# A Fourier filter feeding a gated feed-forward: the order of loads and stores in the prologue, changed

## The chip, the cores and the metric

The kernel runs on one core of one Trainium2 chip. The time is that of the device, in microseconds (us), as the median of several executions. One further execution is recorded by the hardware profiler; its views are what this document reads.

## The reference

The input x has 8 sequences (batches) of 3008 tokens with 256 features. Each feature's sequence goes through a real Fourier transform, is multiplied by a complex filter and is transformed back. The result, 24064 tokens in all, goes through a feed-forward layer with a product of two branches:

```python
X = np.fft.rfft(x, axis=1)
F = (filt_r + 1j * filt_i)[None, :, :]
y = np.fft.irfft(X * F, n=x.shape[1], axis=1)
x = y.reshape(B * S, D)                    # 24064 x 256
gate = np.maximum(x @ w_gate, 0.0)         # 256 -> 1536
val = x @ w_val
out = (gate * val) @ w_out                 # 1536 -> 256
```

## The kernel before

The length 3008 is split as 94 x 32, so that both transforms are matmuls of small tables. For one batch the work goes in four stages.

- **Stage A** (`items_a`, line 269, used for batches 0 and 1). x lies in two SBUF tiles XF[0] and XF[1], 4 MB of room in all, filled by `load_x` (line 172). One item multiplies 512 columns of XF with the table WA in float32 (two passes on PE, line 276) and ScalarE copies the result to a tile asb (line 279). After four items SP stores asb to a DRAM buffer Abuf (line 281). So 16 items make four stores ("quarters"). Batches 2 to 7 take another way: GpSimd loads x in chunks (`load_chunk`), adds and subtracts (`fold_chunk`), and `tiled_a` does smaller matmuls.
- **The bounce.** `load_at` (line 346) reads one quarter of Abuf back, transposed, into a quarter of the tile `at`. A forward transform of the next stage needs all four quarters.
- **Stage B.** `fwd` (line 355) multiplies `at` with the table F2 into PSUM (psX). `product` (line 368) multiplies psX with the filter's parts Ftr and Fti, on VectorE (line 379), or for the pairs in POOL_U by a copy on ScalarE (line 376) and a product on GpSimd (line 377). `inv` (line 382) transforms back with the tables I2t and I2u (line 393), ScalarE copies the result (line 400), and SP stores it to the buffer Dbuf (line 402). For batch 0 this is the loop `first_b`, with six indices i; in it, `amid` puts either filler matmuls or items of stage A of batch 1.
- **Stage C and the feed-forward.** `load_d` (line 421) reads a quarter of Dbuf into dC. `item_c` makes a block yT of 512 tokens. `gv` (line 458) computes val and gate of 128 of the 1536 features, and their product; `o_part` (line 475) multiplies with the output weights. A block takes 12 steps, and there are 47 blocks. Further work is attached to single steps by `at_step` (line 591): step s is feature group s mod 12 of block s div 12.

Every engine runs its instructions in the order in which the program writes them; there is no planner. Stage A and B of batch 1 therefore run where the code puts them: stage A in and after `first_b`, stage B at the steps in the list of line 617, counted from `end`, which is 51 for batch 1.

The prologue needs more than x. The tables I2t and I2u are made on PE from F2 and from the tile `tabs` (`make_back_t`, line 187; `make_back_u`, line 200). The filters are loaded on GpSimd's queue by `load_filters` (line 216, eight transfers, converting to bfloat16) and `load_own_filters` (line 226, the border rows); `place_filter` (line 233) then copies each to a second set of partitions, on VectorE and once on ScalarE. The weights come by `load_vg` (line 244, halves of val and gate) and `load_o`. XF is cleared by memsets first, since x fills only 94 of its rows' groups.

Three devices hold transfers back so that others go first. `hold_gpsimd` (line 255) makes GpSimd copy a few elements of a tile, and so wait for it, before it issues what follows. The load called `last` (line 571) reads the end of Dbuf on GpSimd's queue before the second half of the weights. And the little store `gate` (line 555) makes SP wait for the whole of `at` before it issues the loads of x of batch 1 (line 556).

`warm` (line 504) issues matmuls on a constant tile `junk` whose results nobody reads, to keep TensorE active.

Of the kernel before, what the change touches and what calls it, by code (L numbers as in the profile page):

```python
# [35 lines left out]
def _ap(t, offset_elems, ap_list):  # L36
    return dataclasses.replace(
        t, offset=t.offset + offset_elems, ap=[list(p) for p in ap_list]
    )
# [81 lines left out]
def kernel(  # L121
# [30 lines left out]
    pro = prologue.enter_context(tc.tile_pool(name="pro", bufs=1))  # L152

    Abuf = [dram.tile([NROW * N2, D], BF16, name=f"Abuf{b}") for b in range(B)]
    gate = dram.tile([32, 8], BF16, name="gate")
    Dbuf = [dram.tile([NROW * N2, D], BF16, name=f"Dbuf{b}") for b in range(B)]

    XF = [pro.tile([128, NX2 * D], FP32, name=f"XF{c}") for c in range(N2 // NX2)]
# [13 lines left out]
    def load_x(b, eng, cols):  # L172
        w = NX2 * D
        for c, c0, c1 in cols:
            for m in range(3):
                rows = min(32, B * N1 - (b * N1 + 32 * m))
                eng.dma_start(XF[c][m:m + 4 * rows - 3:4, c0:c1],
                              _ap(x, (b * N1 + 32 * m) * N2 * D + c * w + c0,
                                  [[N2 * D, rows], [1, c1 - c0]]))
# [7 lines left out]
    def make_back_t(q):  # L187

        psI = [ps.tile([128, 4, 64], FP32, tag=fft_tag(), name="psI") for _ in range(2)]
        for e in range(2):  # L190
            for a in range(2):
                for j in range(4):
                    nc.tensor.matmul(psI[e][64 * a:64 * a + 64, j],
                                     F2[64 * e:64 * e + 64, 12 * a + 4 * q + j, :],
                                     perm[64 * e:64 * e + 64], start=True, stop=True,
                                     tile_position=(64 * e, 64 * a))
        for e in range(2):
            nc.vector.tensor_copy(I2t[:, 8 * q + e:8 * q + 8:2, :], psI[e])
# [17 lines left out]
    def load_filters():  # L216

        for src, dst in FILT:
            for a in range(2):
                r, k1, n = a * 64, 1 + 24 * a, NG - 2 * a  # L220
                nc.gpsimd.dma_start(dst[r:r + 31:2, 0:n, :],
                                    _ap(src, k1 * D, [[N1 * D, 16], [1, n * D]]))
                nc.gpsimd.dma_start(dst[r + 1:r + 32:2, 0:n, :],
                                    _ap(src, (N1 - k1) * D, [[N1 * D, 16], [-D, n], [1, D]]))

# [18 lines left out]
    def load_vg(c0, c1):  # L244
        for (w_hbm, w_sb) in ((moe_w_val, WvT), (moe_w_gate, WgT)):
            nc.gpsimd.dma_start(w_sb[:, :, c0:c1],
                                _ap(w_hbm, c0, [[DFF, 128], [128 * DFF, 2], [1, c1 - c0]]))
# [7 lines left out]
    def hold_gpsimd(tile_):  # L255

        scr = sb.tile([128, 8], FP32, tag="scr", bufs=2)
        nc.gpsimd.tensor_copy(scr[:tile_.shape[0]], tile_)  # L258
# [123 lines left out]
    def inv(b, i, tags=None, cuts=CUTS):  # L382

        if i in cuts:
            dsbs[b] = i, sb.tile([128, 2, 4, D], BF16, tag="dsb", bufs=3, name="dsb")
        i0, dsb = dsbs[b]
        psD = [ps.tile([128, 2, D], FP32, tag=tags[a] if tags else fft_tag(), name="psD")
               for a in range(2)]
        for m in range(2):
            for k in range(2):  # L390
                for a in range(2):
                    for e in range(2):
                        nc.tensor.matmul(psD[a][64 * e:64 * e + 64, m],  # L393
                                         (I2t, I2u)[k][64 * a:64 * a + 64, 4 * i + 2 * m + e, :],
                                         tus[b, i, e, k][64 * a:64 * a + 64, m],
                                         start=(k == 0), stop=(k == 1),
                                         tile_position=(64 * a, 64 * e))
        o = 2 * (i - i0)
        for a in range(2):
            nc.scalar.copy(dsb[:, a, o:o + 2, :], psD[a])  # L400
        if i + 1 in cuts:
            nc.sync.dma_start(_ap(Dbuf[b], 2 * i0 * D, [[NG * D, 128], [NG // 2 * D, 2], [1, (o + 2) * D]]),
                              dsb[:, :, :o + 2, :])

    def first_b(amid):

        cuts = (0, 2, 4, 5, 6)
        for i in range(6):
            fwd(0, i)
            if i > 1:  # L410
                inv(0, i - 2, cuts=cuts)
            for e in range(2):
                product(0, i, e, 0)
                product(0, i, e, 1, pool=(i, e) in POOL_U)
            amid(i)
        inv(0, 4, cuts=cuts)
        inv(0, 5, cuts=cuts)

    dCs = {}
# [84 lines left out]
    def warm(n, cols=512):  # L504

        psJ = ps.tile([128, 512], FP32, tag=fft_tag(True), name="psJ")
        for i in range(n):
            nc.tensor.matmul(psJ[:, :cols], junk[:, 0:128], junk[:, :cols], start=True, stop=True)

    nc.sync.dma_start(WA, nc.inline_tensor(wa_h, name="dft_wa").ap())  # L510
    q = NX2 * D // 4
    nc.vector.memset(XF[0][:, 0:q], 0.0)
    nc.gpsimd.memset(XF[0][:, q:2 * q], 0.0)
    nc.vector.memset(junk, 1.0)
# [1 line left out]
    nc.gpsimd.memset(XF[0][:, 3 * q:], 0.0)  # L516
    nc.vector.memset(XF[1][:, 0:2 * q], 0.0)
    nc.gpsimd.memset(XF[1][:, 2 * q:], 0.0)
    load_x(0, nc.sync, ((0, 0, 2 * q), (0, 2 * q, 4 * q), (1, 0, 2 * q)))
    nc.sync.dma_start(F2, nc.inline_tensor(f2_h, name="dft_f2").ap())  # L520
    nc.sync.dma_start(tabs, nc.inline_tensor(tab_h, name="dft_tab").ap())
    load_x(0, nc.sync, ((1, 2 * q, 4 * q),))
    nc.sync.dma_start(WF, nc.inline_tensor(fold_h, name="dft_fold").ap())
    for (src, dst) in FILT:
        nc.vector.memset(dst[64:128, NG - 2:, :], 0.0)
    hold_gpsimd(XF[0][:, 2 * q - 8:2 * q])
    load_filters()
    load_own_filters()

    warm(11)  # L530
    for i, f in enumerate(items_a(0)):
        f()
        if i >= 13:
            make_back_t(i - 13)
        else:
            warm(1, 256)
        if i == 11:
            load_at(0, 0)
    for c in range(1, 4):
        load_at(0, c)  # L540
    for half in range(2):
        for a in range(2):
            place_filter(0, a, half, nc.vector.tensor_copy)
    for i in range(3):
        make_back_u(i)
        warm(6)
    warm(18)
    place_own()
    for half in range(2):
        for a in range(2):  # L550
            place_filter(1, a, half, nc.vector.tensor_copy if a or not half else nc.scalar.copy)
    place_nyq()
    hold_gpsimd(ats[0][0:32, NG - 1, 0:8])
    load_vg(0, DFF // 2)
    nc.sync.dma_start(gate, ats[0][0:32, NG - 1, 0:8])
    load_x(1, nc.sync, ((0, 0, 2 * q), (0, 2 * q, 4 * q), (1, 0, 4 * q)))

    early = items_a(1)
# [1 line left out]
    def amid(i):  # L560
        if i < 2:
            warm(3, 256)
        else:
            for _ in range(2 if i > 2 else 1):
                next(early)()

    turn["tags"], turn["side"] = ("fft", "psv", "psg"), "pso"
    first_b(amid)
    turn["tags"], turn["side"] = ("fft", "psv", "psg", "pso"), None
    load_d(0, 0, 1)  # L570
    nc.gpsimd.dma_start(pro.tile([1, D], BF16, tag="last", bufs=1, name="last"),
                        _ap(Dbuf[0], (N2 * NROW - 1) * D, [[D, 1], [1, D]]))
    load_vg(DFF // 2, DFF)
    load_o()
    for f in early:
        f()
    for h in range(2):
        item_c(0, h)
    prologue.close()
# [11 lines left out]
    def at_step(s, f):  # L591
        side.setdefault(s, []).append(f)

    for s, z in ((0, 1), (9, 2), (14, 3)):
        at_step(s, lambda z=z: load_d(0, z, z + 1))
    C_AT = (8, 10)
    at_step(2, clear_chunks)
    for b in range(1, B):
        end = (b * S // W - 1) * NFT + C_AT[0] - 5
        if b == 1:  # L600
            for c in range(4):
                at_step(3, lambda c=c: load_at(1, c))
        else:
            for j, e in enumerate((-74, -69, -64, -57)):
                l = end - 113 + NFT * j

                def next_x(b=b, j=j, l=l):
                    hold_gpsimd(yTs[l // NFT + 1][:, 0, 0:8])
                    load_chunk(b, j)
                    if j:  # L610
                        fold_chunk(b, j - 1)
                    if j == 3:
                        fold_chunk(b, j)
                at_step(l, next_x)
                at_step(end + e, lambda b=b, j=j: tiled_a(b, j))
            at_step(end + e + 4, lambda b=b: load_at_tiled(b))
        for i, l in enumerate((-35, -28, -25, -22, -16, -11, -4) if b == 1 else
                              (-40, -35, -28, -23, -16, -11, -4)):
            if i < 6:
                at_step(end + l, lambda b=b, i=i: fwd(b, i))  # L620
                for h in range(4):
                    at_step(end + l + h, lambda b=b, i=i, h=h: product(b, i, h // 2, h % 2))
            if i > 0:
                at_step(end + l, lambda b=b, i=i: inv(b, i - 1, ("psv", "psg")))
        at_step(end - 2, lambda b=b: load_d(b))
# [42 lines left out]
```

## Time and profile before

| what | value |
|---|---|
| time, median of 3 | 906.75 us (906.66 to 909.95) |
| the profiled execution | 907.27 us |
| its span | 905.5 us |
| PE busy | 875.3 us, 97% of the span |
| VectorE, ScalarE, GpSimd busy | 566.6, 498.6, 359.0 us |
| PE busy from 0 to 111 us | 92.8 us |
| PE busy from 111 to 905 us | 782.5 of 794 us |
| first matmul of stage A of batch 0 | 7.46 us |
| first forward transform of batch 0 | 33.44 us |
| first matmul of the feed-forward | 63.90 us |

In the profile, PE is TensorE's matmuls and PEld its weight loads, DVE is VectorE, ACT ScalarE, POOL GpSimd, SP SyncE. A name such as `psA L276` is the tile written and the line in the kernel. "DMA at<-Abuf" is the time between the issue of a transfer and its landing. In the windows, "DMA" is the mean busy share of the 16 DMA engines; it goes over 1 where packets overlap.

### The profile page before, as it was taken

Reading aid. Unit: us, or ns where it says so; the run is one execution under the profiler, and the core shown is the slowest. Engines: PE = TensorE matmul, PEld = TensorE weight load, DVE = VectorE, ACT = ScalarE, POOL = GpSimd, SP = SyncE. Lnnn points to the kernel's source line nnn. Section 1 sums busy time; section 2 is a strip of 40 time slices with the busy share of each in tenths; the row PEclk is TensorE's granted clock in tenths of the full one; section 3 lists DMA queues with packets and bytes.
Section 4 is the critical chain, followed back from the end, with each engine's and each line's share of the span. In section 5 each row is a group of like instructions: output and inputs, shape, how many; then the busy total and the mean of one; then the engine's idle time right before and its main releaser. Section 6 shows DMA issues by size and latency. Waiting matters only on the chain.

```text
span 905.5 us, 19111 instructions
## 1 busy us (share of the span) xinstructions
PE 875.3 (97%) x7096; PEld 512.1 (57%) x7217; DVE 566.6 (63%) x872; ACT 498.6 (55%) x891; POOL 359.0 (40%) x351
## 2 busy tenths in 40 slices
PE   8797899999999999999999999999999999999997
PEld 3343565556555665566655566556655556666665
DVE  2635776567665776657766677657766577655553
ACT  4474556555555555555655565655565555555552
POOL 4342667117680386614763166811768000000000
PEclk9899999999999999999999999999999999999999
DMA  9979337623475344663364533754346512331111
GB/s 254 245 219 220 101 95 177 141 80 109 122 175 118 90 126 122 141 134 112 96 161 128 119 98 101 182 116 100 108 136 158 116 31 82 78 75 36 37 32 51
DMA packets 113662, 109.17 MB, mean 121 GB/s; under 512 B 20290, under 2 KB 98370, under 8 KB 112834
## 3 DMA queue, kind: packets, MB, share of 16 engines
q1 hardware_dynamic: 91078, 81.72, 35.3%
q0 software_dynamic: 22176, 26.01, 11.7%
q8 instruction: 57, 0.93, 0.5%
q10 hardware_dynamic: 316, 0.22, 0.1%
q14 instruction: 35, 0.29, 0.1%
HBM read 61.93 MB, written 49.81 MB: 123 GB/s over the span
## 4 chain that ended last, share of the span: by engine, by line
PE 86%; DVE 4%; DMA 4%; ACT 3%; issue 1%; SPq 1%; POOL 0%; DVEq 0%; POOLq 0%
PE psG L464 25%; PE psO L483 25%; PE psV L464 24%; DVE prod L469 4%; PE psA L276 3%; PE psF L322 3%; ACT vsb L467 3%; PE psD L393 2%; PE psX L363 2%; PE psY L448 1%; DMA XF<-in_x_dram 1%; DMA dC<-Dbuf 1%; DMA Abuf<-asb 1%; DMA out_dram<-osb 0%; DMA at<-Abuf 0%
## 5 line engine op out<-in xcount | busy, mean ns | idle before, releaser
L469 DVE SCALAR_TENSOR_TENSOR prod<-psG,vsb 128x512 bf16<-128x512 f32 x564 | 389.0, 690 | 271.3 <-ACT vsb L467 265.8
L467 ACT CAST vsb<-psV 128x512 bf16<-128x512 f32 x564 | 333.0, 590 | 266.8 <-PE psV L464 211.7
L483 PE MATMUL psO<-WoT,prod 128*128 128x256 bf16 x2256 | 336.6, 273 | 1.5
L464 PE MATMUL psG<-yT,WgT 128*128 128x512 bf16 x1099 | 329.1, 379 | 7.4 <-DMA WgT<-in_moe_w_gate_dram 2.5
L464 PE MATMUL psV<-yT,WvT 128*128 128x512 bf16 x1037 | 316.9, 380 | 0.7 <-ACT yT L453 0.4
L483 PEld LDWEIGHTS <-prod 128*128 128x128 bf16 x2256 | 220.7, 98 | 143.4
L464 PEld LDWEIGHTS <-WgT 128*128 128x128 bf16 x1128 | 109.9, 98 | 136.9 <-DMA WgT<-in_moe_w_gate_dram 3.0
L464 PEld LDWEIGHTS <-WvT 128*128 128x128 bf16 x1128 | 98.1, 98 | 41.8 <-issue 30.4
L258 POOL CAST scr<-yT 128x8 f32<-128x8 bf16 x24 | 4.6, 191 | 265.8 <-ACT yT L453 265.8
L379 DVE TENSOR_TENSOR tt<-psX,Ftr 128x512 bf16<-128x512 f32 x96 | 65.0, 682 | 12.9 <-PE psX L363 12.9
L400 ACT CAST dsb<-psD 128x512 bf16<-128x512 f32 x96 | 51.5, 589 | 28.5 <-PE psD L393 28.4
L308 POOL TENSOR_TENSOR fold<-XP 128x1024 f32<-128x1024 f32 x24 | 56.5, 2356 | 25.1 <-PE psF L322 24.9
L489 ACT COPY osb<-psO 128x512 f32<-128x512 f32 x92 | 54.5, 593 | 20.6 <-PE psO L483 20.3
L379 DVE TENSOR_TENSOR uu<-psX,Fti 128x512 bf16<-128x512 f32 x89 | 60.6, 681 | 0.0
L309 POOL TENSOR_TENSOR XP<-XP 128x1024 f32<-128x1024 f32 x24 | 56.4, 2350 | 1.9
L295 POOL DMA_DIRECT2D XP<-in_x_dram x96 | 56.4, 592 | 0.9 <-issue 0.5
L453 ACT CAST yT<-psY 128x512 bf16<-128x512 f32 x47 | 27.6, 586 | 26.2 <-PE psY L448 26.2
L329 DVE CAST asb<-psF 128x512 bf16<-128x512 f32 x48 | 30.9, 686 | 17.3 <-PE psF L322 12.9
L329 ACT CAST asb<-psF 128x512 bf16<-128x512 f32 x48 | 25.8, 589 | 27.3 <-PE psF L322 27.3
L448 PE MATMUL psY<-M,dC 96*128 96x94 bf16 (+18 forms) x604 | 37.7, 198 | 1.1 <-DMA dC<-Dbuf 1.1
L455 DVE CAST yT<-psY 128x512 bf16<-128x512 f32 x47 | 32.0, 681 | 9.8 <-PE psY L448 9.8
L448 PEld LDWEIGHTS <-dC 96*128 96x128 bf16 x604 | 34.5, 97 | 4.6 <-DMA dC<-Dbuf 1.2
(66 smaller groups left out, 481.6 us busy)
## 6 DMA issues: line engine op xcount, KB each, us to landing
at<-Abuf SPq DMA_DIRECT2D x32, 384.0 KB
dC<-Dbuf SPq DMA_DIRECT2D x64, 192.0 KB
XP<-in_x_dram POOLq DMA_DIRECT2D x48, 256.0 KB, 5.9
Dbuf<-dsb SPq DMA_DIRECT2D x23, 512.0 KB
XP<-in_x_dram POOLq DMA_DIRECT2D x96, 96.0 KB, 2.7
Abuf<-asb SPq DMA_DIRECT2D x96, 96.0 KB
out_dram<-osb SPq DMA_DIRECT2D x70, 94.0 KB
XF<-in_x_dram SPq DMA_DIRECT2D x18, 256.0 KB
```

The costliest lines, as they stand in the source:

```text
L295: nc.gpsimd.dma_start(xp[r:r + 24, 0:4:2, :], _ap(x, (b * N1 * N2 + o) * D, [[N2 * D, 24], [47 * N2 * D, 2], [1, 512]]))
L308: tt(t, xp[:, 0:2], xp[:, 2:4], op=ALU.add)
L309: tt(xp[:, 2:4], xp[:, 0:2], xp[:, 2:4], op=ALU.subtract)
L329: copy(asf[:, :, q, :], banks[q])
L379: nc.vector.tensor_tensor(p, psX, filt, op=ALU.mult)
L400: nc.scalar.copy(dsb[:, a, o:o + 2, :], psD[a])
L448: nc.tensor.matmul(psY[:, o:o + w], dCs[b, n2 // 8][:, n2 % 8, h * 128:(h + 1) * 128], M1[:, n1:n1 + w], start=True, stop=True)
L464: nc.tensor.matmul(pt[:, :W], w[:, h, ft * 128:(ft + 1) * 128], yt[:, h, :], start=(h == 0), stop=(h == 1))
L467: nc.scalar.copy(vsb, psV[:, :W])
L469: nc.vector.scalar_tensor_tensor(prod, in0=psG[:, :W], scalar=0.0, in1=vsb, op0=ALU.max, op1=ALU.mult)
L483: nc.tensor.matmul(psO[:, t % 2], prods[ft][:, t * 128:(t + 1) * 128], WoT[:, ft, :], start=(ft == 0), stop=(ft == NFT - 1))
L489: copy(osb[:, t0 % 2:t % 2 + 1], psO[:, t0 % 2:t % 2 + 1])
```

## The change

It touches the prologue and the first steps of the feed-forward.

1. F2 and `tabs` are loaded on ScalarE's queue, at the start. The first filter transfer is issued on GpSimd ahead of its memsets; `load_filters` becomes a generator for this, and its other seven transfers follow when the first half of XF[1] has landed (before: when the first half of XF[0] had).
2. x of batch 0 is loaded in five pieces, the first two of half the size, with nothing between them on SP's queue.
3. Stage A of batch 0 runs without filler and without `make_back_t`, which follows after it with filler of its own.
4. The store `gate` is gone, so that the loads of x of batch 1 stand directly behind the loads of `at` on SP. On GpSimd, the hold on `at` and `load_vg` keep their place.
5. In `first_b`, items of stage A of batch 1 are spread 1, 1, 2, 1, 1 instead of 1, 2, 2, 2, the last one between the last two `inv`.
6. Two quarters of Dbuf are loaded at once, ahead of the other stores to Abuf. The loads of `at` of batch 1 are taken forward: quarter 0 before the rest of stage A, quarter 1 within it, quarters 2 and 3 at steps 0 and 1 (all four were at step 3).
7. The forward transforms of batch 1 stand at steps 11, 16, 23, 28, 35, 40 instead of 16, 23, 26, 29, 35, 40.

```diff
@@ load_filters
                                     _ap(src, k1 * D, [[N1 * D, 16], [1, n * D]]))
+                yield
                 nc.gpsimd.dma_start(dst[r + 1:r + 32:2, 0:n, :],
@@ first_b
         inv(0, 4, cuts=cuts)
+        amid(6)
         inv(0, 5, cuts=cuts)
@@ the prologue
+    q = NX2 * D // 4
     nc.sync.dma_start(WA, nc.inline_tensor(wa_h, name="dft_wa").ap())
-    q = NX2 * D // 4
+    nc.scalar.dma_start(F2, nc.inline_tensor(f2_h, name="dft_f2").ap())
+    nc.scalar.dma_start(tabs, nc.inline_tensor(tab_h, name="dft_tab").ap())
+    filters = load_filters()
+    next(filters)
...
-    load_x(0, nc.sync, ((0, 0, 2 * q), (0, 2 * q, 4 * q), (1, 0, 2 * q)))
-    nc.sync.dma_start(F2, nc.inline_tensor(f2_h, name="dft_f2").ap())
-    nc.sync.dma_start(tabs, nc.inline_tensor(tab_h, name="dft_tab").ap())
-    load_x(0, nc.sync, ((1, 2 * q, 4 * q),))
+    load_x(0, nc.sync, ((0, 0, q), (0, q, 2 * q), (0, 2 * q, 4 * q), (1, 0, 2 * q), (1, 2 * q, 4 * q)))
...
-    hold_gpsimd(XF[0][:, 2 * q - 8:2 * q])
-    load_filters()
+    hold_gpsimd(XF[1][:, 2 * q - 8:2 * q])
+    for _ in filters:
+        pass
     load_own_filters()
 
     warm(11)
     for i, f in enumerate(items_a(0)):
         f()
-        if i >= 13:
-            make_back_t(i - 13)
-        else:
-            warm(1, 256)
         if i == 11:
             load_at(0, 0)
     for c in range(1, 4):
         load_at(0, c)
+    for i in range(3):
+        make_back_t(i)
+        warm(6)
...
     for i in range(3):
         make_back_u(i)
         warm(6)
-    warm(18)
+    warm(6)
...
-    hold_gpsimd(ats[0][0:32, NG - 1, 0:8])
-    load_vg(0, DFF // 2)
-    nc.sync.dma_start(gate, ats[0][0:32, NG - 1, 0:8])
     load_x(1, nc.sync, ((0, 0, 2 * q), (0, 2 * q, 4 * q), (1, 0, 4 * q)))
@@ amid
-            for _ in range(2 if i > 2 else 1):
+            for _ in range((1, 1, 2, 1, 1)[i - 2]):
                 next(early)()
 
+    hold_gpsimd(ats[0][0:32, NG - 1, 0:8])
+    load_vg(0, DFF // 2)
@@ after first_b
-    load_d(0, 0, 1)
+    load_d(0, 0, 2)
...
-    for f in early:
+    load_at(1, 0)
+    for i, f in enumerate(early):
         f()
+        if i == 5:
+            load_at(1, 1)
@@ the steps
-    for s, z in ((0, 1), (9, 2), (14, 3)):
+    for s, z in ((9, 2), (14, 3)):
...
-            for c in range(4):
-                at_step(3, lambda c=c: load_at(1, c))
+            for c in range(2, 4):
+                at_step(c - 2, lambda c=c: load_at(1, c))
...
-        for i, l in enumerate((-35, -28, -25, -22, -16, -11, -4) if b == 1 else
-                              (-40, -35, -28, -23, -16, -11, -4)):
+        for i, l in enumerate((-40, -35, -28, -23, -16, -11, -4)):
```

More of the change, by code (lines that the diff above doesn't have):

```diff
@@ L154 @@
     Abuf = [dram.tile([NROW * N2, D], BF16, name=f"Abuf{b}") for b in range(B)]
-    gate = dram.tile([32, 8], BF16, name="gate")
     Dbuf = [dram.tile([NROW * N2, D], BF16, name=f"Dbuf{b}") for b in range(B)]
```

## The prediction

> **What bounds the kernel now.** I read the chain of waits in order of time first, because the page's totals (PE busy 97% of the span) hide the start. Its first 90 us:
>
> ```profile
> 24.41 5.40 DMA Abuf<-asb
> 29.83 3.48 DMA at<-Abuf
> ...
> 34.98 6.99 DMA XF<-in_x_dram
> ...
> 42.11 1.99 PE psA L276 x2
> ...
> 54.55 7.91 PE psA L276 x18
> ...
> 65.74 9.95 DMA dC<-Dbuf
> ...
> 85.84 1.79 issue
> ```
>
> Columns: start, length, what. Four transfers and a wait stand on the path. Then the windows (start:end, length, then busy time of PE, PEld, DVE, ACT, POOL, then PE clock, DMA share, GB/s):
>
> ```profile
> 0.00:33.40 33.40, 29.37 (x142) 11.37 (x143) 14.30 (x24) 15.11 (x21) 10.58 (x20) 1.00 0.92 254
> ...
> 38.30:42.10 3.80, 0.01 (x2) 0.02 (x1) 0.00 (x0) 2.05 (x4) 2.69 (x3) 0.76 1.11 310
> 42.10:54.60 12.50, 12.49 (x119) 5.34 (x120) 6.26 (x10) 8.56 (x16) 2.43 (x3) 0.80 0.78 281
> ...
> 63.90:87.60 23.70, 18.29 (x98) 8.82 (x100) 12.47 (x19) 10.45 (x18) 9.91 (x11) 1.00 1.17 233
> ...
> 111.00:905.00 794.00, 782.50 (x6467) 469.10 (x6580) 511.79 (x786) 441.54 (x795) 310.42 (x292) 1.00 0.43 108
> ```
>
> After 111 us PE is 98.6% busy and DMA share is 0.43: nothing there changes. All is decided before 111, where DMA is full in three stretches. Last, the list of waits from 63 to 111 us names what holds PE in the feed-forward part:
>
> ```profile
> PE psG L464 <- DMA WgT<-in_moe_w_gate_dram: 2.5, 1, 2.5
> PE psX L363 <- DVE uu L379: 2.2, 2, 1.1
> PE psX L363 <- issue: 1.8, 1, 1.8
> ```
>
> With 0.7 us for dC at 75.8, that is 7.2 us. The "issue" row is the end of the wait for `at` of batch 1: the trace's landing records put its last quarter at 87.54, the matmul at 87.63.
>
> **What the skill says.** "DMA: Bandwidth & Descriptors", section "Issuing engines are not separate DMA queues": another issuing engine saves only the issue time. Here that is 0.59 + 0.43 us of SP for F2 and tabs. Same page, "Queues, rings and completion order": each DMA engine goes round between queues packet by packet. The trace agrees: SP's x and POOL's filters land interleaved from 12 to 20 us. "TensorE: Matmul & The Clock Gate", section "What's actually happening": PE falls to half clock after an idle window of about 3.4 us. The trace agrees: after the 3.8 us wait one item of stage A took 1.99 instead of 0.86; after the 2.5 us wait at 70.1 PE ran on at its old pace.
>
> **Part 1, loads and stage A.** F2 and tabs go from SP's queue (7.76, 8.39) to the head of ACT's (about 0.7). Two issues of some 0.6 us delay ACT's table load (1.28 us); ACT's first copy came at 8.57 after 6.5 us idle, so they cost nothing, unless data came 4 us earlier. The first filter goes ahead of POOL's memsets: 0.65 us later for each (0.95, 0.95, 1.81 us), so the second quarter of XF is clear at about 2.4; SP reaches its load only after three issues of 0.6, at 3.8: hidden. The x loads become 15 instead of 12 issues, +1.8 us of SP, but F2 and tabs (1.0) are gone and the first chunk is half as big. The first three landed at 7.33 before; I put the first 384 KB at 6 and the whole of x at about 14.5 (last issue at 11.4 plus 3), against 18.98.
>
> PE's opening filler, 11 matmuls, runs from 2.53 to 6.85, so stage A starts at 6.9 instead of 7.46. Each item is 2 x 0.43; the 13 fillers (0.11 each) and the three groups of make_back_t (0.28 to 0.35) leave. 16 x 0.86 = 13.8, so the last item ends at 20.7 and its copy (0.59) at 21.3 instead of 24.39: -3.1.
>
> This is not yet gain. The other seven filters now wait at line 258 for half of XF[1] (about 12.2, against 7.5). Eight landed between 14.2 and 27.9, the border filter at 28.12; DVE's fourth copy waited for that one (28.21), and from there to its last copy at 32.9 are 4.7 us. With less x beside them seven may land by 26.5, or, at the same pace, by 30: copies end at 31.2 to 34.7. `at` I put at 31 (same bytes, DMA full some 1.5 us sooner, and no lone tail such as 29.83 to 33.31). PE's fillers after stage A, 42 at 0.214, and the table work (3 x 0.35 + 3 x 0.38) end at 31.9. I take the first product (33.89 before) at 33.4: **-0.5**.
>
> **Part 2, x of batch 1.** The gate store is gone, and these nine loads follow the last `at` load in SP's queue instead of waiting for it to land; val/gate stay behind the bounce on POOL. The first data came 4.5 us after issue, at 38.31, and the third transfer at 41.97. Queued ahead, 768 KB right behind `at` at the 254 GB/s of the window is 3 us: 34. PE wants it at about 37.5. So the 3.8 us wait goes: **-3.8**. At half clock, 42.11 to 45.5 cost 3.5 us for work worth 1.7; I keep half of that loss: **-0.9**. Of the items of stage A inside the loop, 6 instead of 7 come before inv(5). From 45.5 to 54.55 took 9.05 us; now DVE's ten remaining products (0.68) bound it at about 7.5: **-1.5**. The loop ends at 47.9 instead of 54.55. Then ten items instead of nine (+0.86): the feed-forward starts at 57.9 instead of 63.9, in sum **-6.0**.
>
> **Part 3, after the start (T).** Both first quarters of dC go ahead of three Abuf stores: the 0.7 wait at 75.8 goes. gate's second half: its issue stands to T as before, I keep 2.2 of 2.5. The forward transforms of batch 1 move from steps 16, 23, 26, 29, 35, 40 to 11, 16, 23, 28, 35, 40: four products (4 x 0.68) and the steps' own 0.69 fitted badly into three steps of 1.3 us; that 2.2 us of waits on DVE goes. But step 11 comes at about T+13, and `at` of batch 1 must be there. Before, it landed 28.9 us after the last store of D (58.64). Now its four loads go in as each store lands, the first ahead of the stores, instead of behind all of them: landing order D, D, at, two stores, at, store, at, at. At 1.9 us a store and 2.7 to 3 a load, as in the records between 67 and 87, I get 22 to 25 us after the last store (51.8): 74 to 77. The wait is 3 to 6; I take 4.0, and 0.5 for a cold clock. Sum: 2.2 + 4.0 + 0.5 = 6.7 against 7.2: **-0.5**. SP's loads of dC 2 and 3 stand behind `at`, and next_x at step 10 brings 768 KB beside it from about T+15: in the range.
>
> Total -6.5: the profiled execution, 907.27 (span 905.5 and 1.8 around it), becomes 900.8. It lies 0.5 above the median 906.75, so I say 900.5.
>
> **Rivals.** (1) *The filters become the wait.* For: they start 4.7 us later, and DVE's copies stand in order ahead of the first product. Landing at 31 puts that product at 35.7, the loop's end at 50, T at 60; `at` comes at 79, step 12 then starts near 80 against 79.4, and with 1.8 and 2.2 of later waits gone the time is some 3.5 lower: 903.3. Against: eight needed 17.6 us beside x, and x is gone early. (2) *The transform at step 11 waits for `at` as long as it did at step 16.* For: DMA share is 1.17 there and the bytes are the same. PE runs in order, so all behind step 11 waits too. Landing again at 87.5, step 12 starts 8.1 later than at 79.4, +0.9 of cold clock, -4.0 for the two waits: +5, 912. It decides from a landing at 82.5; below that the change is no loss. Against: the stores of batch 1 are out 5 to 6 us earlier. (3) *It doesn't do what it says*: x of batch 1 fights with `at` or the filters, and the product starts late by as much as the wait saved: 906.
>
> **Chances.** 60% for the forecast, its own range 896 to 902.2. 25% for rivals 1 and 3 together (903 to 907). 15% for rival 2 and its like (909 and above). A measurement of this kernel tells about 0.5% (4.5 us) from no change, so faster means below 902.2, slower above 911.3; half of rival 2's weight stays below that, but a clock lost in the longer waits, or idle PE before the first product, can do the same, so I leave 0.13 there. The range 895 to 909 takes in rivals 1 and 3 and the filters' bounds, and leaves some 2 in 10.
>
> **What will show it.** Stage A without gaps from 6.9 to 20.7; the fourth copy of Ftr at 26.5 to 30; no DMA XF piece in the chain near 40; the feed-forward's first psV at 57 to 59; one wait of 3 to 6 us on psX at step 11; no psX waits on DVE uu after it. The forecast is wrong if `at` of batch 1 lands after 80, or the first product starts after 35.

## The result, and the profile after

The changed kernel takes 913.99 us (median of 4, 911.72 to 914.88) against 906.7 (906.28 to 909.95): a ratio of 1.0069, 95% interval 1.0039 to 1.0098. It is slower by 7.3 us, where 6 us less was forecast. The profiled execution took 913.64 us, its span 911.9.

The chain of waits of the changed kernel, in order of time (start, length, what), shows one old wait gone and a much longer one at the end:

```profile
23.07 8.68 DMA Abuf<-asb
...
31.82 3.57 DMA at<-Abuf
...
40.78 1.95 PE psA L276 x2
...
52.42 8.77 PE psA L276 x20
...
73.37 6.64 DMA Abuf<-asb
80.03 0.58 SPq L349
...
81.33 6.87 DMA dC<-Dbuf
88.22 0.64 PE psX L363 x8
```

The 6.99 us of `XF` near 35 are gone: x of batch 1 is there when PE wants it. The bounce before it has grown, from 5.40 + 3.48 to 8.68 + 3.57. And from 73.4 to 88.22 PE does nothing. The windows of the same execution (start:end, length, busy time of PE, PEld, DVE, ACT, POOL, then PE clock, DMA share, GB/s) show how much that is:

```profile
38.30:42.10 3.80, 2.70 (x16) 0.91 (x13) 2.06 (x4) 1.92 (x4) 2.71 (x3) 0.50 1.00 290
42.10:54.60 12.50, 12.23 (x121) 5.10 (x121) 6.26 (x10) 10.98 (x22) 4.58 (x4) 0.92 0.86 268
...
63.90:87.60 23.70, 9.53 (x54) 4.31 (x52) 8.67 (x13) 6.86 (x12) 8.42 (x10) 0.81 1.09 223
```

In the last stretch PE was busy for 18.29 us before and is for 9.53 now, while the DMA engines are nearly as full (1.17 before, 1.09). The list of waits names the place, with total, count and longest:

```profile
PE psX L363 <- DMA dC<-Dbuf: 14.8, 1, 14.8
```

The name of the transfer is not to be trusted here. psX reads `at`, not dC. By the trace's landing records the last quarter of `at` landed at 87.97, and the two transfers of dC behind it at 88.46 and 89.24: the view picks one that was under way when the wait ended. PE stands at step 11 for the last quarter of `at` of batch 1, whose landing before was 87.54. PE began the feed-forward 1.6 us earlier and then met a transfer that came 0.4 us later, five steps sooner in its own order.

What SP and GpSimd did meanwhile stands in the timeline of the changed kernel, first SP's queue, then GpSimd's:

```profile
58.02 0.62 SPq L349 DMA_DIRECT2D at<-Abuf  x1
58.68 4.97 SPq L281 DMA_DIRECT2D Abuf<-asb  x2
72.66 0.61 SPq L349 DMA_DIRECT2D at<-Abuf  x1
73.37 0.58 SPq L281 DMA_DIRECT2D Abuf<-asb  x1
74.05 6.56 SPq L349 DMA_DIRECT2D at<-Abuf  x2
...
71.30 0.19 POOL L258 CAST scr<-yT 128x8 f32<-128x8 bf16 x1 [2.97 <-ACT yT L454]
71.53 2.40 POOL L295 DMA_DIRECT2D XP<-in_x_dram  x4
```

Two things are seen. SP is silent from 63.65 to 72.66: the load of quarter 1 waits for its store to land (72.64), and the last store, whose data ScalarE had ready by 62, stands behind it until 73.37. And GpSimd asks for the first chunk of x of batch 2 (896 KB by the trace's own sizes: the four issues shown of 96 KB and two more of 256 KB; the 768 KB given for it in the prediction and for e5_x_later is too low) at 71.53, just before the last three quarters of `at` are asked for, at 72.66, 74.05 and 80.03. In the kernel before, the chunk stands behind the four loads of `at` (SP's queue, then GpSimd's):

```profile
66.63 10.65 SPq L349 DMA_DIRECT2D at<-Abuf  x4
...
76.78 0.19 POOL L258 CAST scr<-yT 128x8 f32<-128x8 bf16 x1 [6.98 <-ACT yT L453]
77.01 2.40 POOL L295 DMA_DIRECT2D XP<-in_x_dram  x4
```

There the last of the four loads was asked for at 74.10, 2.9 us before the chunk. Which of these two, and the earlier step, cost the time is what the runs had to tell.

### The profile page after: what moved, and what is told of

The parts are those of the page before. It is cut to its first block, busy times and chain, and to the rows that moved or that the text cites. A ratio compares the mean times of both kernels' runs of the same rounds, so it can differ in the third digit from the quotient of the medians.

```text
span 911.9 us, 19220 instructions
## 1 busy us (share of the span) xinstructions
PE 882.3 (97%) x7210; PEld 512.7 (56%) x7210; DVE 566.2 (62%) x872; ACT 498.2 (55%) x891; POOL 358.4 (39%) x351
## 4 chain that ended last, share of the span: by engine, by line
PE 94%; DMA 4%; SPq 1%; ACT 0%; POOL 0%; issue 0%; DVE 0%; ACTq 0%; POOLq 0%
PE psV L465 28%; PE psG L465 27%; PE psO L484 26%; PE psF L322 3%; PE psA L276 3%; PE psD L393 3%; PE psY L449 2%; PE psX L363 2%; DMA Abuf<-asb 2%; DMA dC<-Dbuf 1%; DMA out_dram<-osb 1%; SPq L176 1%; DMA XF<-in_x_dram 0%; DMA at<-Abuf 0%; POOL uu L377 0%
## 5 line engine op out<-in xcount | busy, mean ns | idle before, releaser
L465 PE MATMUL psV<-yT,WvT 128*128 128x512 bf16 x1128 | 337.0, 380 | 0.7 <-ACT yT L454 0.7
L465 PE MATMUL psG<-yT,WgT 128*128 128x512 bf16 x1128 | 335.8, 379 | 0.0
L363 PE MATMUL psX<-at,F 64*64 64x256 bf16 x384 | 20.3, 287 | 17.1 <-DMA dC<-Dbuf 14.8
```

Of the source, the lines that this page charges most:

```text
L465: nc.tensor.matmul(pt[:, :W], w[:, h, ft * 128:(ft + 1) * 128], yt[:, h, :], start=(h == 0), stop=(h == 1))
```

## The experiments

The kernel before was timed again beside each group of runs; its medians were 906.2 to 906.5 us.

**Which part costs: the list of steps undone.**

```diff
-        for i, l in enumerate((-40, -35, -28, -23, -16, -11, -4)):
+        for i, l in enumerate((-35, -28, -25, -22, -16, -11, -4) if b == 1 else
+                              (-40, -35, -28, -23, -16, -11, -4)):
```

> The changed kernel with part 7 undone: the forward transforms of batch 1 again at steps 16, 23, 26, 29. Theory A (PE, in order, stands at step 11 until the last quarter of at of batch 1 lands at 88): the landing stays at 86 to 89, the wait moves to step 16, which PE reaches about 6.8 us of work later, near 80; the wait is 7 to 8 us instead of 15, some 2 us of waits on DVE come back, and the time is 908 to 910. Theory B (the loads are late because DMA is full of what PE's progress sets off): the landing moves too, by 4 us or more, and the time stays at 912 to 915.

909.78 us, ratio 1.0027 (1.0005 to 1.0049). The last quarter landed at 87.52, the wait moved to step 16 and was 6.5 us. Theory A held, with a wait a little shorter than its 7 to 8 us. So part 7 costs the changed kernel some 4 us, and 3.5 remain without it.

**The list alone, on the kernel before.** The same edit the other way round.

> The kernel before with part 7 alone: the forward transforms of batch 1 at steps 11, 16, 23, 28. Theory A: at lands at 87 to 88 as before, PE waits at step 11 (reached at 79.4) for 7 to 9 us, 1 to 2 us go to the cold clock after it, 1.8 and 2.2 us of later waits go; the time is 910 to 913. Theory B (the list costs nothing by itself): 904 to 907.

913.08 us, ratio 1.0064 (1.0047 to 1.0082). PE waited 11.0 us at step 11; in this execution, at 917.1 us one of the two longest of the run's 20, the last quarter landed at 90.5. Theory A held, a little worse than its numbers. The list is a loss by itself, since nothing lets `at` come earlier.

**The prologue alone.** Parts 1 to 5, with the loads of D and `at` and the list as before.

```diff
-    load_d(0, 0, 2)
+    load_d(0, 0, 1)
...
-    load_at(1, 0)
-    for i, f in enumerate(early):
+    for f in early:
         f()
-        if i == 5:
-            load_at(1, 1)
...
-    for s, z in ((9, 2), (14, 3)):
+    for s, z in ((0, 1), (9, 2), (14, 3)):
...
-            for c in range(2, 4):
-                at_step(c - 2, lambda c=c: load_at(1, c))
+            for c in range(4):
+                at_step(3, lambda c=c: load_at(1, c))
...
-        for i, l in enumerate((-40, -35, -28, -23, -16, -11, -4)):
+        for i, l in enumerate((-35, -28, -25, -22, -16, -11, -4) if b == 1 else
+                              (-40, -35, -28, -23, -16, -11, -4)):
```

> Parts 1 to 5 alone: the new prologue, with the loads of D and of at of batch 1 and the list of steps as before. Theory A: the feed-forward starts 1 to 2 us earlier than at 63.9, as in the changed kernel (62.3), the rest follows at its old distance, and the time is 904 to 906. Theory B (the prologue itself costs, since the first product came 2.2 us later): 907 to 910.

903.87 us, ratio 0.9967 (0.9952 to 0.9982): theory A. The feed-forward began at 62.98 in its profile, the last quarter of `at` landed at 84.08, and there was no wait of note at step 16. The prologue is worth 2.4 us, and the whole loss lies behind it.

**Is it the blocked store?** The changed kernel with the load of quarter 1 moved behind all stores.

```diff
-    for i, f in enumerate(early):
+    for f in early:
         f()
-        if i == 5:
-            load_at(1, 1)
+    load_at(1, 1)
```

> The changed kernel with one move: the load of quarter 1 of at of batch 1 comes after all of stage A's items, not after the sixth. Theory A (head of line: in SP's queue the load waits for its store to land, from 63.7 to 72.7, and the last store, ready at 62, stands behind it until 73.4): the last store is issued at about 63 to 65, its quarter lands at 79 to 83 instead of 88, the wait at step 11 falls from 15 to 6 to 10 us, the time to 905 to 909. Theory B (DMA is full, the order in SP's queue matters little): the last quarter lands at 86 or later and the time stays at 912 or more.

913.11 us, ratio 1.0054 (1.0037 to 1.0071), no better. The last store did go out at 61.92 instead of 73.37, and landed at 73.8 instead of 80.0. But the last quarter, asked for at 73.83, landed only at 86.66, 12.8 us later. My first theory (A) fell here, and B's numbers came: the blocked store is real, but not what set the landing.

**Is it the chunk of x of batch 2?** A third theory: PE comes to step 10 sooner, so the chunk is asked for sooner, and shares the engines with the last quarters. The first try of it wrote the request seven steps later.

```diff
-                at_step(l, next_x)
+                at_step(17 if (b, j) == (2, 0) else l, next_x)
```

> The run e2_order and one more move: the first chunk of x of batch 2 (768 KB on GpSimd's queue) is asked for at step 17 instead of step 10. Theory C (this chunk, issued at 71.6 because PE reached step 10 early, shares the DMA engines with the last three quarters of at, 71 to 86): without it the last quarter lands at 78 to 82.5 instead of 86.7, the wait at step 11 falls from 13.4 to 5 to 9 us, the time from 913 to 904 to 909. Theory B (the stores, at, weights and dC fill DMA anyway): the last quarter lands at 85 or later, the time stays at 911 or more.

912.86 us, ratio 1.006 (1.0047 to 1.0073), and the chunk was still asked for at 72.23. GpSimd had no other instruction to wait for, and ran ahead to the one moved. The run says nothing of the theory. The next one makes the chunk wait for what it should follow, by reading `at`:

```diff
-                    hold_gpsimd(yTs[l // NFT + 1][:, 0, 0:8])
+                    hold_gpsimd(ats[1][0:32, NG - 1, 0:8] if (b, j) == (2, 0) else yTs[l // NFT + 1][:, 0, 0:8])
```

> The run e2_order, with the first chunk of x of batch 2 held on GpSimd until at of batch 1 has landed (in e5_x_later the chunk was only written later; GpSimd had nothing ahead of it and still asked for it at 72.2, so that run did not test this). Theory C (the chunk shares the DMA engines with the last quarters of at): the last quarter lands at 78 to 82.5 instead of 86.7, PE waits 5 to 9 us at step 11 instead of 13.4, the time is 904 to 909 instead of 913. Theory B (without it the engines are as full): the last quarter lands at 85 or later, the time stays at 911 or more.

906.48 us, ratio 0.9999 (0.9983 to 1.0015): 6.6 us off e2_order by this one hold. The last quarter landed at 81.16, 5.0 us after its issue. PE's timeline of e2_order has the wait at step 11 (in brackets) without the hold; the list of waits of this run, then GpSimd's timeline, have it with the hold:

```profile
86.90 0.64 PE L363 MATMUL psX<-at,F 64*64 64x256 bf16 x8 [13.37 <-DMA at<-Abuf]
...
PE psX L363 <- DMA at<-Abuf: 8.1, 1, 8.1
...
81.37 0.18 POOL L258 CAST scr<-at 32x8 f32<-32x8 bf16 x1 [13.16 <-DMA at<-Abuf]
81.92 2.40 POOL L295 DMA_DIRECT2D XP<-in_x_dram  x4 [0.37 <-POOL scr L258]
```

Theory C held. The chunk went out 10.3 us later than in e2_order, and PE did not wait for it. How the two shared the engines can be read from the queues: from the request of quarter 1 to the landing of the last, SP's queue moved 2.10 MB in 15.4 us in e2_order and 1.59 MB in 7.6 us here, 136 against 209 GB/s, while GpSimd's (the chunk and the end of the output weights) took 44% of the engines' time there and 4% here.

**The same hold on the changed kernel itself**, with the blocked store left in.

> The changed kernel with one edit: the first chunk of x of batch 2 held on GpSimd until at of batch 1 has landed. If this chunk alone makes the quarters late: the last one lands at 80 to 83 instead of 88, the wait at step 11 falls from 14.8 to 6 to 9 us, the time from 914 to 906 to 909. If the blocked last store (issued at 73.4 behind the load of quarter 1) counts as much: the last quarter lands at 84 to 86 and the time is 910 to 912.

906.82 us, ratio 1.0006 (0.9993 to 1.0019). The last store went out at 72.81 as before, but now landed in 4.4 us, and the last quarter in 3.8 after its own request, at 81.05. The wait at step 11 was 7.8 us, where the changed kernel has 14.8:

```profile
81.30 0.64 PE L363 MATMUL psX<-at,F 64*64 64x256 bf16 x8 [7.81 <-DMA at<-Abuf]
```

The first expectation held. With the chunk out of the way the blocked store made no difference to the time that these runs can tell.

**Which half of part 6 brings the chunk forward.** The run e4_prologue with both first quarters of D loaded at once, and nothing else.

```diff
-    load_d(0, 0, 1)
+    load_d(0, 0, 2)
...
-    for s, z in ((0, 1), (9, 2), (14, 3)):
+    for s, z in ((9, 2), (14, 3)):
```

> The run e4_prologue with one half of part 6: both first quarters of D loaded at once, ahead of the stores to Abuf; the loads of at of batch 1 stay at step 3. If the order of the loads of at was the costly half: the 2.1 us wait for dC at 74.6 goes, the last quarter of at lands within 1.5 us of 84.1, the time is 902 to 904.5. If loading D first is the costly half, since it puts 384 KB ahead of the three stores: the stores and the last quarter land 3 us later or more, PE waits at step 16, and the time is 907 or more.

909.86 us, ratio 1.0031 (1.0018 to 1.0044): 6 us worse than without it. I had expected a loss, if any, from stores delayed behind D. They were not: the last store landed at 71.6 against 70.7. The wait for dC at 74.6 (2.1 us) went, and that for the weights fell from 1.1 to 0.6, so PE came to step 10 sooner; another 0.9 us is an earlier start of the feed-forward in this execution (62.06 against 62.98). The wait for dC and the chunk in e4_prologue, then the chunk and the wait for `at` in this run:

```profile
PE psY L449 <- DMA dC<-Dbuf: 2.1, 1, 2.1
75.79 2.40 POOL L295 DMA_DIRECT2D XP<-in_x_dram  x4
...
71.98 2.40 POOL L295 DMA_DIRECT2D XP<-in_x_dram  x4
...
PE psX L363 <- DMA at<-Abuf: 6.3, 1, 6.3
```

The chunk was asked for at 71.98 instead of 75.79, and the last quarter, asked for at about the same time as in e4_prologue (71.6 and 72.2), landed at 87.46 instead of 84.08. A wait of 2 us taken away brought one of 6.3. (The two profiled executions are only 3.2 us apart, 908.69 and 905.53; the 6 us are from the medians.) What counts is the chunk's place behind the quarters, not its time: in e8_spaced, below, it was asked for as early, at 72.10, but the last quarter had been asked for at 68.42 and landed at 82.04.

**What in the prologue gains.** The kernel before without the gate store.

```diff
-    gate = dram.tile([32, 8], BF16, name="gate")
...
-    nc.sync.dma_start(gate, ats[0][0:32, NG - 1, 0:8])
```

> The kernel before without the gate store, nothing else. Theory A (the 3.8 us wait for x of batch 1 is owed to the gate): x is issued at 30.5 to 31.5 instead of 33.8, its third transfer lands before 38.5 instead of 41.97, the wait falls below 1 us, the feed-forward starts 2 to 4 us before 63.9, and the time is 902.5 to 905. Rival (x then slows at and the border filters, so that the first product comes as much later): 905.5 to 908.

903.33 us, ratio 0.9967 (0.9947 to 0.9987): as good as all of parts 1 to 5 together. x was asked for at 31.01, its third transfer landed at 37.52, and the feed-forward began at 59.88. Theory A held; of the rival's effect there is little, `at` of batch 0 landed 0.6 us later than before (33.91). In its chain the bounce takes as long as in the kernel before, and the item of stage A follows the products directly:

```profile
24.86 5.46 DMA Abuf<-asb
...
30.34 3.56 DMA at<-Abuf
...
36.05 2.29 POOL uu L376 x2
...
38.38 0.52 PE psD L392 x11
38.90 1.56 PE psA L275 x2
```

**Do the late filters cost?** The run e4_prologue with the filters released by the first half of XF[0] again.

```diff
-    hold_gpsimd(XF[1][:, 2 * q - 8:2 * q])
+    hold_gpsimd(XF[0][:, 2 * q - 8:2 * q])
```

> The run e4_prologue with the filters held, as in the kernel before, only until the first half of XF[0] has landed. Theory A (the seven filters take some 14 us whatever goes beside them, so their start sets the first product): they are issued from about 9 instead of 14.8, the border filter lands at 26 to 29 instead of 30.7, the first product comes at 33 to 35 instead of 36.1, the time is 901 to 903. Rival (what the filters gain, x and the bounce lose: at lands at 35 or later and holds the first product): 903.5 to 905.5.

905.39 us, ratio 0.999 (0.9977 to 1.0002), 1.5 us more than e4_prologue. The filters were asked for from 9.6, but the border filter landed at 29.68, a gain of only 1.3 us (30.94 in e4_prologue). The rival's time came, but only half by its path. x was slower: it had all landed at 20.85 instead of 16.93, and the last store of stage A went out at 25.38 instead of 23.07. The bounce did not hold the first product, for `at` landed at 34.79, sooner than in e4_prologue (36.03). VectorE did: its casts of `make_back_t` follow stage A, its copies of the filters follow the casts, and the copies ran from 29.20 to 37.35 almost without a pause. The first product came at 37.39 (36.72 in e4_prologue).

**Does the spacing of the transforms help where `at` is there?**

```diff
-        for i, l in enumerate((-35, -28, -25, -22, -16, -11, -4) if b == 1 else
+        for i, l in enumerate((-35, -30, -25, -20, -15, -10, -4) if b == 1 else
```

> The run e4_prologue with the forward transforms of batch 1 at steps 16, 21, 26, 31, 36, 41 (before: 16, 23, 26, 29, 35, 40): none earlier than at is there, and five steps for each four products. Theory A (spacing alone was the good in part 7): the waits of psX on DVE, 2.2 us in the kernel before, go and nothing comes in their place; 901 to 902.5. Rival (the waits only move to a later step): 903.5 to 905.

904.79 us, ratio 0.9971 (0.9956 to 0.9985), no gain over e4_prologue. The rival held: psX no longer waited on DVE, but two matmuls of stage C did (`psY` on `uu`, 3.1 us in all), since they take the same PSUM buffers and now stood next to a transform.

**A version from these findings**: the kernel before, without the gate store, with both first quarters of D loaded at once, and with the chunk held until `at` has landed. Three edits that stand above.

> Made of what the runs showed to help or not to harm, on the kernel before: no gate store, both first quarters of D loaded at once, and the first chunk of x of batch 2 held until at of batch 1 has landed; list of steps and the rest as before. If the three add up: the feed-forward starts at 60 to 61, no wait for dC, none for at at step 16, 900 to 902.5. If the chunk that is held is then missed later, or the quarters of D only move the wait to the weights: 903 to 905, no better than without the gate store alone.

899.77 us (898.61 to 900.8), ratio 0.9916 (0.989 to 0.9941), just under the range expected if the three add up. The feed-forward began at 59.44, the last quarter of `at` landed at 79.79, before step 16, and neither dC nor `at` was waited for. The windows of this run over the same stretch, and the largest wait for a transfer left to PE's weight loads, from the list of waits from 63 to 111 us (the matmul behind it waited 1.8 us, and one for the output weights 0.5):

```profile
63.90:87.60 23.70, 21.16 (x139) 11.45 (x137) 15.27 (x24) 11.87 (x21) 6.00 (x10) 1.00 0.96 213
...
PEld L463 <- DMA WgT<-in_moe_w_gate_dram: 2.3, 1, 2.3
```

PE is busy for 21.16 us of 23.70, against 18.29 before and 9.53 in the changed kernel, at fewer GB/s than before: part of the chunk now moves after this stretch (it is whole only at 94.86). All three kernels load and store the same data; when each transfer goes is the difference. Loading D first, which cost 6 us in e10_d_first, does no harm that shows once the chunk is held. No run holds the chunk with D loaded as before, so the 3.6 us gained over e6_no_gate are not divided between the two. The times of the main runs, from the landing records and the timeline:

| run | chunk asked for | last quarter asked for | landed | wait for it (step) | time |
|---|---|---|---|---|---|
| before | 77.0 | 74.1 | 87.5 | 1.8 (16) | 906.7 |
| changed | 71.5 | 80.0 | 88.0 | 14.8 (11) | 914.0 |
| e2_order | 71.6 | 73.8 | 86.7 | 13.4 (11) | 913.1 |
| e9_x_held | 81.9 | 76.1 | 81.2 | 8.1 (11) | 906.5 |
| e12_after_held | 81.8 | 77.2 | 81.1 | 7.8 (11) | 906.8 |
| e1_list | 72.4 | 83.2 | 87.5 | 6.5 (16) | 909.8 |
| e3_list_alone | 77.7 | 74.8 | 90.5 | 11.0 (11) | 913.1 |
| e4_prologue | 75.8 | 72.2 | 84.1 | none over 0.5 (16) | 903.9 |
| e10_d_first | 72.0 | 71.6 | 87.5 | 6.3 (16) | 909.9 |
| e6_no_gate | 73.3 | 70.7 | 83.0 | 1.0 (16) | 903.3 |
| e8_spaced | 72.1 | 68.4 | 82.0 | 1.3 (16) | 904.8 |
| e11_best | 80.1 | 70.1 | 79.8 | none (16) | 899.8 |

## Why the prediction was wrong

**The step that failed** is the landing of `at` of batch 1 in part 3: "I get 22 to 25 us after the last store (51.8): 74 to 77. The wait is 3 to 6". It landed at 87.97, and the wait was 14.8. Both terms of that sum were short. The last store of D landed at 56.01, 4.2 us later than the 51.8, which parts 1 and 2 below explain. And from there to the landing of `at` it took 32.0 us, 7 more than the 25. Both signs of being wrong that the prediction names came: `at` after 80, and the first product, at 36.08, after 35.

The second term is the chunk of x of batch 2. With it held, the same distance was 25.0 us (e12_after_held, 56.05 to 81.05) and 25.3 (e9_x_held, 55.89 to 81.16), the upper end of the forecast. The prediction priced it at nothing beyond its range: "next_x at step 10 brings 768 KB beside it from about T+15: in the range". It was asked for at 71.53, which is T+9.2 (T+13.1 in the kernel before), ahead of three of the four quarters. I had just taken away the waits for dC and for the weights, on the path to step 10, and did not carry the gain forward to the request that step 10 makes. By the clock the request came only 1.4 us before 57.9 + 15; the rest is that the loads of `at`, which it was to follow, were themselves late.

The hold was worth 6.6 us in e9_x_held and 7.2 in e12_after_held. It does not bring the forecast back: 906.8 is no gain, for PE, standing at step 11, still waited 7.8 us for an `at` that landed at 81 instead of 74 to 77. Of the 13.5 us between the 900.5 forecast and the 914.0 measured, 4.4 came with the start of the feed-forward and 10.8 with the wait (14.8 against 4.0); the 2.2 kept for the wait on the weights did not come, and the rest is 0.5.

**Rival 2 is what happened**, with its sign and its size: a landing at 87.5 was to give 912, and a landing at 88.0 gave 914. Its turning point, 82.5, was fair too: landings at 81.1 and 81.2 gave 906.5 and 906.8, no loss. I gave it 15% on the ground that the stores of batch 1 would be out 5 to 6 us earlier. They were not, for the loop of stage B ended only about 2 us earlier, and the last store was held back behind the load of quarter 1 to 73.37 against 63.09. I had the order of the loads and stores right, but not that a load which waits for its store keeps all that follows on SP; by e2_order and e12_after_held this slip did not cost time that shows.

**Part 1** was forecast at -0.5; the first product came at 36.08 instead of 33.89, +2.2. Stage A had a gap of 1.37 us at 10.5 for the third piece of x and ended at 22.44, not 20.7. SP's fifteen issues are in the chain there: the halves cost as much to issue as whole pieces (0.59 us). The seven filters, asked for from 14.84 instead of 12.2, took until 30.7. What held the first product was `at`: put at 31, it landed at 35.39, for the last store of stage A took 8.68 us instead of 5.40. VectorE's copies ended at 35.50, past the 34.7 of the forecast, so the filters alone would have held the product nearly as long. In the stretch from 8 to 24 us the engines moved 258 GB/s, against 294 before. It may be that the filters' short rows ran slower without the large ones of x beside them, or only that nothing new was asked for between 12.6 and 14.8 us; no run separates the two. Rival 1 was therefore half right: the border filter came at 30.7, close to its 31. But e7_hold shows that starting the filters earlier gains nothing either, since stage A, and VectorE's copies behind it, then come later.

**Part 2** was right on its main term: without the gate the wait for x is gone, and e6_no_gate alone gives the 2 to 4 us at which that run was expected. The half of the cold clock that I took as saved was not: the first item of stage A took 1.95 us in the changed kernel, 1.99 before. Of the -6.0 forecast at the start of the feed-forward, -1.6 came (62.33 against 63.90). Part 1 is 2.7 of the missing 4.4 (+2.2 instead of -0.5); the loop with its cold clock took 1.8 us longer than forecast, from the first product at 36.08 to its end at 52.42. (The prediction's own terms give -5.8, not -6.0.)

**Part 3** otherwise: the waits for the weights and dC were gone, and so were those of psX on DVE. These 5.4 us were more than eaten by the one wait at step 11: some 7 us of it go when the chunk is held, and 7.8 stay, because the transform stands five steps earlier than before.

Summed up from the runs: the prologue -2.4 (e4_prologue), D first with its consequence +6.0 (e10_d_first against it), the other order of the loads of `at` about 0 (e1_list against that), the list of steps +4.2 (the changed kernel against e1_list). That is +7.7 from the medians, and +7.3 with the kernel before as timed beside the changed one. The steps lead from the one kernel to the other, so they have to add up; what each is worth holds for this order.

## What to carry to other kernels

When a wait is taken away, follow the engine to the next transfer that its progress sets off, and ask what is in the queues then. A request tied to a step of compute moves with the compute; if it must come after another transfer, tie it to that transfer's landing. And a consumer moved forward in an in-order engine gains only if its data also come earlier; otherwise everything behind it waits as well.

## What the runs showed that I had not expected

The last quarter of `at` (384 KB in rows of 512 bytes) landed 12.8 us after its issue in e2_order and 5.0 us after it in e9_x_held, where only the chunk on the other queue was held: two and a half times as late. The time from issue to landing does not show this by itself. The first quarter of e10_d_first took 13.3 us, of which 10 passed before the chunk was asked for, and the last of e11_best, with the chunk held, 9.7: these stood behind other transfers of SP's own queue.

Moving an instruction later in the program did not delay it on an engine that had nothing else to do in between: the request written at step 17 went out at 72.23, the one at step 10 at 71.62.

The start of the feed-forward differs between executions of one prologue: 62.98 in e4_prologue, 60.28 in e8_spaced, with PE clocks of 0.89 and 1.00 granted between 33 and 63 us. The medians hardly differ (903.9 and 904.8). A step of 2 us in a single profile was therefore not taken as proof of anything here without the times beside it. Why the clock was granted in one and not in the other is open.
